# Weights of a tap product side by side in SBUF: a new layout for the tap factors of an S4 convolution kernel

## The chip, the cores and the metric

The kernel runs on one core of a Trainium2 chip. The metric is the device time of one execution in microseconds (us), as the median of several runs. A second number: the mean granted clock of the matmul engine (TensorE, "PE" in the profile). It is read from a record in the trace, as a share of full speed. In the records it takes only two values, 1.0 and 0.5. It begins late, 27.1 us after the first instruction in the kernel before, and the profile counts the time before that as full clock. So all mean clocks and half-clock times below say nothing about the first 30 us or so.

Some terms: SBUF is the on-chip memory that holds the operands, and PSUM the one to which matmuls write their sums. In the profile DVE is the vector engine, ACT the scalar engine, PE a matmul (of a moving operand, whose columns are counted below, with weights loaded before) and PEld the loading of its weights.

Runs of one kernel differ by up to 3%. A run is called slow when it is more than 1.5% above the fastest run of the same kernel. Ratios here use fast runs only.

## The reference, cut to what matters

The reference normalises the input, and runs a diagonal state-space model (S4) as a long convolution. It adds an expert's output for one routed token, applies a gate and adds the residual. The part that this change touches is the generation of the convolution kernel `K`:

```python
logdA = dt * A                              # A complex, (512, 128)
P = jnp.exp(logdA[:, :, None] * l)          # l = 0 .. 2047
K = jnp.einsum("dn,dnl,dn->dl", Cc, P, dB).real
# ... y = irfft(rfft(xn) * rfft(K)) + xn * Dskip
```

The kernel writes the exponential as a product of a factor for a small step (32 steps) and a factor for a large one (20 of them). The factors for the small steps are a table `QQ`, and those for the large steps, together with `C` and `dB`, a table `GG`. Both have the 128 states on the partitions. A matrix product of the two, summed over the states, gives taps of `K`: one such tap product has as its 128 weights the 32 small steps of 4 channels (one channel `jj` of each of the four groups `gp`), and as its 80 moving columns the 20 large steps of the same 4 channels. The exponents of the small steps are themselves made on PE, as outer products of the rows of `dt * A` (a row is a channel) with the numbers 0.5 to 15.5.

## The kernel before

All matmuls are issued through one helper, so the profile gives them all the line L187; its groups are told apart by the names of the operands. A matmul is written `(output in PSUM, weights, moving operand, start, stop)`. `sap(tensor, first partition, partitions, offset, [[step, count], ...])` is an access pattern along the free dimension, in elements. `PB` is the PSUM (float32, 4 bytes an element). The other operands are bfloat16, 2 bytes an element.

The outer products, in 16 calls of `args` (8 from `exps`, 8 from `qgen`):

```python
IDIJ[pp, :, pp % 32] = np.arange(16) + 0.5      # table [128, 16, 32]: 16 numbers, each 32 times to pick a row (channel)

def args(pi, c, pair):
    q, js = c // 2, c % 2
    rs = slice(32 * q, 32 * q + 32)             # 32 rows of the array
    for gp in range(4):
        o = PB[:, 2 * pair + gp // 2, 256 * (gp % 2):256 * (gp % 2) + 256]
        for hl in range(2):                     # high and low half of dt*A
            mms.append((o, AD[rs, pi, hl, gp, :], IDIJ[rs, :, 16 * js:16 * js + 16], hl == 0, hl == 1))
```

One call is 8 matmuls of 256 columns. The moving operand runs over 16 neighbouring elements (32 bytes) at a time, and the PSUM write is contiguous. In the result the channel is the innermost index, so `QQ` has the shape `[128, 2, 2, 4, 32, 16]`, which ends in group, step and channel `jj`.

The tap products, in 8 calls of `kgen` with 32 matmuls each:

```python
mms.append((PB[:, bank, 80 * k:80 * k + 80],
            sap(QQ, 0, 128, 4096 * qb + 2048 * ci + jj, [[16, 128]]),          # weights: step 16 elements, 32 bytes
            sap(GG, 0, 128, 2560 * ci + 16 * js + jj, [[32, 4], [128, 20]]), ci == 0, ci == 1))   # moving: step 256 bytes
```

The weights of one tap product lie 32 bytes apart. That is what the change is about. Two more groups: `PB<-KT,W` (640 matmuls of the spectrum of `K`) and `PB<-PAB,FA` (512 matmuls of the inverse transform). Both have contiguous weights and a contiguous moving operand.

The kernel issues a few matmuls on constants (`PB<-CA`, from L280) for the sole purpose of keeping PE busy. They are called fillers below.

## Time and profile before

| | before |
|---|---|
| median of 3 runs | 224.8 us (224.78 to 227.97) |
| span and granted clock of the profiled run | 222.4 us, 0.899 |
| PE busy | 188.2 us, 85% of the span |

The page of the kernel before has the busy time of each engine, the granted clock in 40 equal slices (tenths, 9 is 90% or more), and the shares of the engines in the chain of work that ended last:

```profile
PE 188.2 (85%) x2399; PEld 142.4 (64%) x2407; DVE 143.9 (65%) x339; ACT 143.9 (65%) x186; POOL 14.0 (6%) x24
...
PEclk9999999999696769766999999855599999999969
...
PE 54%; DVE 20%; ACT 12%; DMA 7%; issue 2%; SPq 2%; POOL 0%; DVEq 0%; ACTq 0%
```

PE is the busiest engine and leads the chain. A slice is 5.56 us. The clock drops in two places, between about 55 and 105 us (several slices of 6 and 7) and between about 140 and 161 us (8, 5, 5, 5), and once more for 3.4 us near the end. As the clock is either 1.0 or 0.5, a mean of 0.899 means that the record holds (1 - 0.899) / 0.5 * 222.4 = 45 us at half clock. The 9s of the first slices are not measured. The first outer products tell that the clock was low there:

```profile
6.79 3.59 PE L187 MATMUL PB<-CA,AD 32*128 32x256 bf16 x16 [6.79 <-DVE AD L738]
```

They start every 213 ns, as the same matmuls do at half clock later; at full clock it is 109 ns.

The groups view of the kernel before gives, after the bar, busy time in us and the mean ns of one instruction, then the idle time before the group:

```profile
L187 PE MATMUL PB<-KT,W 128*128 128x128 bf16 x640 | 41.3, 222 | 0.8 <-ACT K2T L754 0.3 <-issue 0.2
L187 PE MATMUL PB<-GG,QQ 128*128 128x80 bf16 x256 | 40.3, 326 | 0.7 <-ACT KT L754 0.7
...
L187 PEld LDWEIGHTS PB<-GG,QQ 128*128 128x128 bf16 x256 | 35.7, 147 | 3.1 <-ACT KT L754 1.4 <-issue 0.8
L187 PE MATMUL PB<-CA,AD 32*128 32x256 bf16 x128 | 21.5, 323 | 7.5 <-DVE AD L738 6.8 <-ACT EE L754 0.7
...
L725 DVE TENSOR_TENSOR QQ<-QQ,EE 128x2048 bf16<-128x2048 bf16 x16 | 19.5, 1219 | 0.1
L187 PE MATMUL PB<-PAB,FA 64*128 64x128 bf16 x512 | 17.2, 217 | 2.9 <-DVE PAB L725 2.4 <-ACT ZT L754 0.5
...
L725 DVE TENSOR_TENSOR KP<-GG,QQ 128x128 bf16<-128x128 bf16 x8 | 1.8, 221 | 18.4 <-PE PB L187 18.4
```

A busy time of 41.3 us for 640 matmuls is 65 ns apiece; 222 ns is the time from start to end of one. They overlap in time: at full clock one starts every 56 ns. Dividing the busy time by the number is therefore the way to read the rate: 157 ns for each tap product of 80 columns, 65 ns for each spectrum matmul of 128 columns.

The timeline of PE in the kernel before (start, length, group) shows the rate within one burst:

```profile
97.46 1.97 PE L187 MATMUL PB<-GG,QQ 128*128 128x80 bf16 x12
99.25 0.74 PE L187 MATMUL PB<-KT,W 128*128 128x128 bf16 x10
```

Twelve tap products take 99.25 - 97.46 = 1.79 us, 149 ns each, where spectrum matmuls with more columns start every 56 ns at full clock. The tap products also start every 147 to 150 ns in a stretch (150 to 157 us) where the granted clock is 0.5. So what limits them didn't slow down with the PE clock here.

The timeline of the same kernel, later, shows one call of outer products between two groups:

```profile
111.68 1.04 PE L187 MATMUL PB<-CA,AD 32*128 32x256 bf16 x8
112.65 2.41 PE L187 MATMUL PB<-KT,W 128*128 128x128 bf16 x40
```

The call takes 112.65 - 111.68 = 0.97 us.

The windows view of the kernel before gives the busy time and number of instructions of each engine in a stretch, then the granted clock, the share of DMA and GB/s. These are two of the five stretches that the trace was cut into:

```profile
62.00:107.00 45.00, 44.44 (x457) 35.76 (x459) 22.80 (x45) 24.29 (x38) 0.05 (x1) 0.77 0.41 155
107.00:140.00 33.00, 30.33 (x545) 24.06 (x544) 31.16 (x65) 31.71 (x36) 1.18 (x1) 1.00 0.52 144
```

From 107 to 140 us PE, DVE and ACT are all busy for 30 to 32 of 33 us, at full clock. PE time that is added there can hardly be hidden.

### The profile page before, as it was taken

How to read it: one execution, taken by the hardware profiler on the slowest of the kernel's cores; microseconds unless marked ns; L12 is line 12 of the kernel's file. 1: busy time of each engine (PE TensorE's matmuls, PEld its weight loads, DVE VectorE, ACT ScalarE, POOL GpSimd, SP SyncE). 2: the span in 40 equal slices, each digit the busy share in tenths (PEclk: the TensorE clock that was granted, in tenths of full speed). 3: DMA queues.
4: the chain of work that ended last, by engine and by line, in shares of the span. 5: the costliest groups of instructions: out<-in, count | busy, mean ns of one | idle time of the engine just before them, and what ended most of it. 6: DMA issues, size and time to landing. Idle time of an engine off the chain costs nothing.

```text
span 222.4 us, 5535 instructions
## 1 busy us (share of the span) xinstructions
PE 188.2 (85%) x2399; PEld 142.4 (64%) x2407; DVE 143.9 (65%) x339; ACT 143.9 (65%) x186; POOL 14.0 (6%) x24
## 2 busy tenths in 40 slices
PE   0683987975899999999999978899999999997290
PEld 0453575753277768878877755777676989986030
DVE  3899923799960399640599999823889821434273
ACT  2597798557634679342997999643778535566821
POOL 0090000020110000000000002002000300000000
PEclk9999999999696769766999999855599999999969
DMA  6899920289799733000026576748200091377875
GB/s 178 300 367 388 425 120 3 76 239 328 196 411 425 286 89 103 1 3 0 3 62 176 168 184 213 210 135 199 82 3 1 12 216 31 80 165 233 197 170 138
DMA packets 40666, 36.79 MB, mean 165 GB/s; under 512 B 26593, under 2 KB 35938, under 8 KB 39746
## 3 DMA queue, kind: packets, MB, share of 16 engines
q1 hardware_dynamic: 38178, 22.25, 35.4%
q0 software_dynamic: 2464, 14.19, 17.9%
q8 instruction: 19, 0.31, 0.6%
q14 instruction: 5, 0.04, 0.1%
HBM read 25.95 MB, written 10.49 MB: 164 GB/s over the span
## 4 chain that ended last, share of the span: by engine, by line
PE 54%; DVE 20%; ACT 12%; DMA 7%; issue 2%; SPq 2%; POOL 0%; DVEq 0%; ACTq 0%
PE PB L187 51%; DMA WD<-in_B_w_down_dram 4%; DVE PAB L725 4%; DMA X<-in_A_u_dram 3%; ACT K2T L754 3%; DVE TT L725 3%; ACT XT L957 3%; PE PB L280 2%; DVE T L725 2%; DVE ST L802 2%; ACT AT L754 2%; DVE TF L725 2%; SPq L210 2%; ACT QQ L754 1%; DVE GG L725 1%
## 5 line engine op out<-in xcount | busy, mean ns | idle before, releaser
L187 PE MATMUL PB<-KT,W 128*128 128x128 bf16 x640 | 41.3, 222 | 0.8 <-ACT K2T L754 0.3
L187 PE MATMUL PB<-GG,QQ 128*128 128x80 bf16 x256 | 40.3, 326 | 0.7 <-ACT KT L754 0.7
L187 PEld LDWEIGHTS PB<-KT,W 128*128 128x128 bf16 x640 | 37.2, 99 | 4.7 <-ACT K2T L754 2.1
L187 PEld LDWEIGHTS PB<-GG,QQ 128*128 128x128 bf16 x256 | 35.7, 147 | 3.1 <-ACT KT L754 1.4
L754 ACT ACTIVATE KT<-PB 128x400 bf16<-128x400 f32 (+2 forms) x32 | 15.7, 500 | 26.4 <-PE PB L187 26.4
L187 PE MATMUL PB<-CA,AD 32*128 32x256 bf16 (+1 forms) x192 | 24.4, 309 | 8.2 <-DVE AD L738 7.4
L725 DVE TENSOR_TENSOR PAB<-U,K2T 128x1024 bf16<-128x1024 bf16 x32 | 21.0, 686 | 14.6 <-ACT K2T L754 14.6
L725 DVE TENSOR_TENSOR TT<-GG,ZB 128x512 bf16<-128x512 bf16 (+2 forms) x64 | 27.7, 470 | 0.7
L187 PEld LDWEIGHTS PB<-CA,AD 32*128 32x128 bf16 x192 | 15.5, 114 | 15.4 <-DVE AD L738 7.6
L754 ACT ACTIVATE K2T<-PB 128x1024 bf16<-128x1024 f32 x16 | 16.4, 1024 | 8.0 <-PE PB L187 8.0
L754 ACT ACTIVATE AT<-PB 128x1024 bf16<-128x1024 f32 x16 | 15.8, 1021 | 8.3 <-PE PB L187 6.6
L754 ACT ACTIVATE U<-PB 128x1024 bf16<-128x1024 f32 x16 | 16.4, 1022 | 7.0 <-PE PB L187 6.9
L187 PE MATMUL PB<-PAB,FA 64*128 64x128 bf16 x512 | 17.2, 217 | 2.9 <-DVE PAB L725 2.4
L725 DVE TENSOR_TENSOR QQ<-QQ,EE 128x2048 bf16<-128x2048 bf16 x16 | 19.5, 1219 | 0.1
L187 PEld LDWEIGHTS PB<-PAB,FA 64*128 64x128 bf16 x512 | 14.4, 94 | 5.3 <-DVE PAB L725 2.7
L754 ACT ACTIVATE ZT<-PB 128x1024 bf16<-128x1024 f32 x16 | 16.4, 1027 | 1.5 <-PE PB L187 1.5
L725 DVE TENSOR_TENSOR GG<-TT 128x512 bf16<-128x512 bf16 (+2 forms) x32 | 15.1, 473 | 0.8
L754 ACT ACTIVATE EE<-PB 128x1024 bf16<-128x1024 f32 x16 | 15.4, 1023 | 0.2
L187 PE MATMUL PB<-XN,CB 128*128 128x256 bf16 (+1 forms) x80 | 11.9, 280 | 4.2 <-ACT AT L754 2.8
L187 PE MATMUL PB<-BT,F2T 128*64 128x256 bf16 x128 | 13.7, 354 | 0.5 <-ACT K2T L754 0.5
L725 DVE TENSOR_TENSOR KP<-GG,QQ 128x128 bf16<-128x128 bf16 x8 | 1.8, 221 | 18.4 <-PE PB L187 18.4
L187 PE MATMUL PB<-DD,CB 128*128 128x512 bf16 x32 | 10.3, 416 | 3.4 <-DVE KV L725 2.9
(130 smaller groups left out, 235.3 us busy)
## 6 DMA issues: line engine op xcount, KB each, us to landing
W<-c_w POOLq DMA_DIRECT2D x4, 1280.0 KB, 12.5
scr_a<-AT SPq DMA_DIRECT2D x8, 512.0 KB, 6.2
BT<-scr_a SPq DMA_DIRECT2D x8, 512.0 KB, 5.7
scr_z<-ZT SPq DMA_DIRECT2D x16, 256.0 KB, 2.9
DD<-scr_z SPq DMA_DIRECT2D x6, 512.0 KB, 5.2
XR<-in_A_u_dram POOLq DMA_DIRECT2D x4, 512.0 KB, 6.1
out_dram<-XR SPq DMA_DIRECT2D x8, 256.0 KB, 2.6
X<-in_A_u_dram SPq DMA_DIRECT2D x3, 512.0 KB, 6.8
```

The costliest lines, as they stand in the source:

```text
L187: fns.append(lambda e, o=o, l=l, r=r, st=st, sp=sp, tp=tp: e.matmul(o, lhsT=l, rhs=r, start=st, stop=sp, tile_position=tp, skip_group_chec ...
L210: fns.append(lambda e, dst=dst, src=src: e.dma_start(dst, src))
L280: n.fns = [lambda e, o=o: e.matmul(o, lhsT=lhs, rhs=rhs, start=True, stop=True, tile_position=(0, 0), skip_group_check=True)] * k
L725: g.V(lambda e: e.tensor_tensor(out=o, in0=a, in1=b, op=op), [o], [a, b], n, mode)
L754: nd = g.A(lambda e: e.activation(out=o, in_=i, func=func, **kw), [o], ins, n + (110 if "bias" in kw else 0), after=[ph["pre"]] if tab els ...
L802: g.V(lambda e, b=b: e.bn_stats(ST[:, b, :], X0[:, b, :]), [ST[:, b, :]], [X0[:, b, :]], 512)
L957: g.A(lambda e, pv=pv, xt=xt: e.activation(out=xt, in_=pv, func=ACT.Copy), [XT[:, bq % 2]], [PB[:, bank, :]], 1024)
```

## The change

The intent is to have the 128 weights of one tap product side by side, so that they load without a step. `QQ` becomes `[128, 2, 2, 64, 32]`, where 64 is channel `jj` by group and 32 is the step; the 4 * 32 weights of one `jj` are now neighbours. To write `QQ` in that order without a transposition, the outer products must deliver their results channel by channel, with the steps innermost. Hence 16 matmuls of 128 columns in place of 8 of 256, and a moving operand whose neighbouring elements are 64 bytes apart in the unchanged table `IDIJ`.

```diff
--- before.py
+++ after.py
@@ -668,7 +668,7 @@
         EE = place("EE", [128, 9, 1024], BF16)
         AD = place("AD", [128, 2, 2, 4, 128], BF16)
         o_q = cur[0]
-        QQ = place("QQ", [128, 2, 2, 4, 32, 16], BF16)
+        QQ = place("QQ", [128, 2, 2, 64, 32], BF16)
         WW0 = place("WW0", [128, 2, 256], F32, o_q + 8192)
         ZB0 = place("ZB0", [128, 256], F32, o_q + 8192 + 2048)
         o_g = cur[0]
@@ -850,16 +850,17 @@
             rs = slice(32 * q, 32 * q + 32)
             mms = []
             for gp in range(4):
-                o = PB[:, 2 * pair + gp // 2, 256 * (gp % 2):256 * (gp % 2) + 256]
-                for hl in range(2):
-                    mms.append((o, AD[rs, pi, hl, gp, :], IDIJ[rs, :, 16 * js:16 * js + 16], hl == 0, hl == 1))
+                for h in range(2):
+                    o = sap(PB, 0, 128, 512 * (2 * pair + h) + 16 * gp, [[64, 8], [1, 16]])
+                    for hl in range(2):
+                        mms.append((o, AD[rs, pi, hl, gp, :], IDIJ[rs, :, 16 * js + 8 * h:16 * js + 8 * h + 8].rearrange("p k j -> p j k"), hl == 0, hl == 1))
             g.M(mms)
-            return PAIR4[pair]
+            return PAIR[pair].rearrange("p a b -> p (a b)")
 
         def exps(c, pair=0):
             src = args(0, c, pair)
             for s in range(2):
-                act(EE[:, 2 * (c % 4) + s, :].rearrange("p (a b) -> p a b", a=4), src, ACT.Exp, 1024, scale=(-8.0 if s == 0 else 8.0))
+                act(EE[:, 2 * (c % 4) + s, :], src, ACT.Exp, 1024, scale=(-8.0 if s == 0 else 8.0))
 
         g.sec = "pow"
         for jb in range(2):
@@ -1027,14 +1028,15 @@
             bf = c % 2
 
             def qv(s):
-                return QQ[:, bf, :, :, 16 * s:16 * s + 16, :].rearrange("p x a b c -> p x a (b c)")
-
+                return QQ[:, bf, :, :, 16 * s:16 * s + 16]
+
+            src = src.rearrange("p (a b) -> p a b", b=16)
             e0 = 2 * (c % 4)
             act(qv(1)[:, 0], src, ACT.Sin, 1024, scale=-8.0, bias=HPI)
             act(qv(1)[:, 1], src, ACT.Sin, 1024, scale=8.0)
             ts(EE[:, 8, :], EE[:, e0 + 1, :], -1.0, MUL, 1024, 4)
-            tt(qv(0), qv(1), EE[:, e0, :].rearrange("p (a b) -> p a b", a=4)[:, None].to_broadcast([128, 2, 4, 256]), MUL, 2048, 2)
-            ep = EE[:, e0 + 1:9:7 - e0, :].rearrange("p x (a b) -> p x a b", a=4)
+            tt(qv(0), qv(1), EE[:, e0, :].rearrange("p (a b) -> p a b", b=16)[:, None].to_broadcast([128, 2, 64, 16]), MUL, 2048, 2)
+            ep = EE[:, e0 + 1:9:7 - e0, :].rearrange("p x (a b) -> p x a b", b=16)
             tt(qv(1), qv(1), ep, MUL, 2048, 2)
 
         def gchain(q):
@@ -1064,14 +1066,14 @@
                 for k in range(nj):
                     jj = j0 + k
                     for ci in range(2):
-                        mms.append((PB[:, bank, 80 * k:80 * k + 80], sap(QQ, 0, 128, 4096 * qb + 2048 * ci + jj, [[16, 128]]),
+                        mms.append((PB[:, bank, 80 * k:80 * k + 80], sap(QQ, 0, 128, 4096 * qb + 2048 * ci + 128 * jj, [[1, 128]]),
                                     sap(GG, 0, 128, 2560 * ci + 16 * js + jj, [[32, 4], [128, 20]]), ci == 0, ci == 1))
                 g.M(mms)
                 act(KT[:, j0:j0 + nj].rearrange("p a b c -> p (a b c)"), PB[:, bank, 0:80 * nj], ACT.Copy, 80 * nj)
                 j0 += nj
             kp = KP[:]
             gl = GG[:, 0, :, 19, :].rearrange("p x (g s j) -> p x g s j", g=4, s=2)[:, :, :, js, :]
-            tt(kp, gl, QQ[:, qb, :, :, 31, :], MUL, 128, 1)
+            tt(kp, gl, sap(QQ, 0, 128, 4096 * qb + 31, [[2048, 2], [32, 4], [128, 16]]), MUL, 128, 1)
             mms = []
             for gp in range(4):
                 for m in range(4):
```

## The prediction

> **What bounds the kernel now.** The chain of waits puts 51% of the span on the matmul helper line; PE is busy 85% (page, part 1). The change touches three streams.
>
> 1. Tap products (PB<-GG,QQ, 256 pairs). In the timeline they start every 147 to 150 ns; the 640 pairs PB<-KT,W, whose weights and moving operand are both contiguous, start every 56 ns. The group view shows the weight load at 147 ns against 99. That suggests the strided weights, but neighbouring instructions say otherwise: the last GG matmul before a KT,W matmul (contiguous weights) still holds it back 137 to 138 ns, and a strided QQ load behind a KT,W matmul delays nothing (56 ns). At a burst's start the next load begins 44 ns after a strided one, 15 ns after a contiguous one. So the moving operand GG, 80 columns 256 B apart, sets about 1.7 ns per column, and the strided weights add only about 11 ns. The 149 ns also holds where the granted clock is 0.50 (150 to 157 us), so the limit is in time, not in PE clocks.
> 2. The KT matmuls, moving stride 160 B, agree: a 64-column one holds its successor 101 to 108 ns. The KP matmuls, contiguous moving and a PSUM step of 16 B, follow in 28 ns for 64 columns.
> 3. Step outer products (PB<-CA,AD, 128 matmuls of 256 columns): moving runs of 16 elements, 110 ns at full clock, 213 at half.
>
> **What the change does.** It makes the tap weights contiguous: I expect 137 ns instead of 148, 256 x 11 ns = 2.8 us less PE, nearly all critical. But the outer products become 256 matmuls of 128 columns whose moving operand steps 64 B every column. [...] The 160 B and 256 B streams agree, at 1.6 to 1.7 ns per column; no stream of this trace moves at 64 B, but the weight load at 32 B is slowed too. My estimate is 215 ns per new matmul at either clock: a call of outer products takes 3.44 us instead of 0.88 (1.7 at low clock). DVE and ACT write 16-element runs instead of 256: KP reads such runs in 221 ns today, so I expect no change; KP itself loses some 60 ns.
>
> **Critical path, by calls.** First four calls: PE becomes the limit, 4 x 3.44 us from 6.8 us; ACT reaches the layernorm's logarithm at about 24.5 instead of 19.9: +4.6. Call at 38 us, inside the router's chain: +2.4. Call at 51.7: hidden before the WD load. Calls at 77 and 85: +1.8, +2.4. Stretch 107 to 140 us: PE 30.3, DVE 31.2, ACT 31.7 of 33 us busy; six calls add 15.4 to PE, gaps absorb about 2.6: +12.8. Calls at 154 and 165: +1.8, +2.6. Sum +28.4, less 2.8: about +25.6. I add a little for lower granted clock.
>
> **Prediction: 251 us, range 242 to 262; faster 0.04, same 0.04, slower 0.92.**
>
> **What would show it.** PB<-CA,AD matmuls starting 215 ns apart; their busy time near 55 us instead of 21.5; GG matmuls 135 to 140 ns apart, their weight loads near 100 ns; QQ TENSOR_TENSOR still about 1.22 us; PE, not DVE, leading the chain between 110 and 140 us.
>
> **What would make it wrong.** If a 64 B step runs at full rate, the outer products stay near 56 ns per 128 columns and the result is about 222 us. If GG pairs fall toward 60 ns, the weight load was the limit after all, worth up to 20 us. [...]

The 215 ns stand as an estimate from the streams of the trace: at the 1.58 to 1.71 ns a column of the 160- and 256-byte steps, 128 columns take 202 to 219 ns.

## The result and the profile after

| | before, same rounds | after |
|---|---|---|
| median | 224.79 us (4 runs, 222.51 to 227.97) | 266.92 us (4 runs, 263.08 to 267.96) |
| ratio of fast runs | | 1.18, 95% interval 1.158 to 1.205 |
| span and clock of the profiled run | 222.4 us, 0.899 | 266.0 us, 0.775 |

A ratio is the mean time of one kernel's fast runs over that of the other's fast runs of the same rounds, so it isn't quite the ratio of the medians quoted. The output was correct, here and in every experiment below.

The kernel is slower, as predicted, but by 42 us (by the medians; 41 us by the fast runs) instead of 26. The result is outside the predicted range. The profiled run of the kernel after (267.52 us) counts as slow; its two fast runs took 263.08 and 266.32 us at a clock of 0.821 and 0.793. Every run of the kernel after, fast or slow, had a lower clock than 0.83, so the low clock isn't a trait of the profiled run alone. As that run is 2.8 us above the mean of the two fast ones, the times of its trace below are a little too high.

The page of the kernel after, same lines:

```profile
PE 240.1 (90%) x2527; PEld 164.6 (62%) x2535; DVE 145.6 (55%) x339; ACT 145.4 (55%) x186; POOL 14.0 (5%) x24
...
PEclk9999998557965589779795559556558799799957
...
PE 81%; ACT 11%; DVE 3%; DMA 2%; issue 1%; SPq 0%; DVEq 0%; ACTq 0%
```

PE gained 52 us of busy time and leads 81% of the chain. The row of the clock has changed more than anything else: half clock is now spread over the whole run from the seventh slice on. It adds up to (1 - 0.775) / 0.5 * 266.0 = 120 us. The mean clocks of the two fast runs give 94 and 110 us in the same way.

The groups of the kernel after:

```profile
L187 PE MATMUL PB<-CA,AD 32*128 32x128 bf16 x320 | 59.6, 367 | 7.1 <-DMA CA<-c_ca 7.1
L187 PE MATMUL PB<-KT,W 128*128 128x128 bf16 x640 | 49.8, 246 | 1.0 <-issue 0.3 <-ACT K2T L754 0.3
...
L187 PE MATMUL PB<-GG,QQ 128*128 128x80 bf16 x256 | 37.6, 314 | 0.7 <-ACT KT L754 0.7
...
L187 PEld LDWEIGHTS PB<-GG,QQ 128*128 128x128 bf16 x256 | 28.9, 117 | 7.1 <-ACT KT L754 1.4 <-issue 1.1
...
L187 PE MATMUL PB<-PAB,FA 64*128 64x128 bf16 x512 | 20.8, 242 | 1.4 <-DVE PAB L725 1.4
L725 DVE TENSOR_TENSOR QQ<-QQ,EE 128x2048 bf16<-128x2048 bf16 x16 | 19.5, 1220 | 0.6 <-ACT QQ L754 0.4
...
L725 DVE TENSOR_TENSOR KP<-GG,QQ 128x128 bf16<-128x128 bf16 x8 | 3.0, 369 | 17.1 <-PE PB L187 17.1
```

The group `PB<-CA,AD 32x128` now holds 64 matmuls of another step (the powers, 3.9 us before) as well as the 256 new outer products. The outer products grew from 21.5 to about 59.6 - 3.9 = 55.7 us. Tap products fell from 40.3 to 37.6 us. The surprise is in the second and the fifth line: `PB<-KT,W` grew from 41.3 to 49.8 us and `PB<-PAB,FA` from 17.2 to 20.8 us, though the change doesn't touch them.

The timeline of the kernel after, at the place that was shown of before:

```profile
111.70 1.81 PE L187 MATMUL PB<-GG,QQ 128*128 128x80 bf16 x12
113.33 0.74 PE L187 MATMUL PB<-KT,W 128*128 128x128 bf16 x10
```

Twelve tap products now take 1.63 us, 136 ns each. And the calls of outer products, with the group behind them:

```profile
125.49 3.62 PE L187 MATMUL PB<-CA,AD 32*128 32x128 bf16 x16
129.05 4.03 PE L187 MATMUL PB<-KT,W 128*128 128x128 bf16 x40
...
134.20 2.41 PE L187 MATMUL PB<-KT,W 128*128 128x128 bf16 x40
```

A call takes 129.05 - 125.49 = 3.56 us, or 223 ns a matmul with the handover; inside the burst they start every 216 ns. The 40 spectrum matmuls that follow took 2.41 us before and take 4.03 us here. The next 40, at 134.20, take 2.41 us again: the same instructions, at another clock (0.5 in the record from 129.25 to 132.66 us, 1.0 from there to 139.49 us).

Windows of the kernel after, for the corresponding stretches:

```profile
71.40:121.00 49.60, 48.95 (x480) 35.08 (x481) 23.47 (x45) 24.95 (x39) 0.41 (x1) 0.72 0.36 134
121.00:176.20 55.20, 55.08 (x587) 37.88 (x582) 31.89 (x66) 32.73 (x35) 1.18 (x1) 0.70 0.37 101
```

The busy stretch of 33.0 us has become 55.2 us, in which PE is busy all but 0.1 us and the granted clock is 0.70. With the five stretches of both traces, cut at the same events, the gain and loss by stretch is as follows:

| stretch in before, us | before | after | change | predicted |
|---|---|---|---|---|
| 0 to 21 | 21.0 | 24.8 | +3.8 | +4.6 |
| 21 to 62 | 41.0 | 46.6 | +5.6 | +2.4 |
| 62 to 107 | 45.0 | 49.6 | +4.6 | +2.8 |
| 107 to 140 | 33.0 | 55.2 | +22.2 | +12.8 |
| 140 to 222.4 | 82.4 | 89.8 | +7.4 | +3.0 |

(The predicted column puts half of the 2.8 us gained by the tap products into each stretch that has them.) The early stretch, which the record of the clock doesn't reach, came out slightly better than predicted. Each of the others came out worse; their recorded clock is 0.78, 0.72, 0.70 and 0.79 after, against 0.96, 0.77, 1.00 and 0.87 before.

The groups with contiguous operands that the change left alone explain where PE time appeared from: `KT,W` +8.5, `PAB,FA` +3.6, `XN,CB` +3.0, `DD,CB` +2.2, `BT,F2T` +0.8 and the fillers +1.5 us of busy time. That is 19.6 us. The tap products, which start every 136 to 139 ns in the kernel after at full and at half clock alike, show no such growth.

### The profile page after: what moved, and what is told of

The parts are those of the page before. It is cut to its first block, busy times and chain, and to the rows that moved or that the text cites. A ratio compares the mean times of both kernels' runs of the same rounds, so it can differ in the third digit from the quotient of the medians.

```text
span 266.0 us, 5791 instructions
## 1 busy us (share of the span) xinstructions
PE 240.1 (90%) x2527; PEld 164.6 (62%) x2535; DVE 145.6 (55%) x339; ACT 145.4 (55%) x186; POOL 14.0 (5%) x24
## 4 chain that ended last, share of the span: by engine, by line
PE 81%; ACT 11%; DVE 3%; DMA 2%; issue 1%; SPq 0%; DVEq 0%; ACTq 0%
PE PB L187 78%; ACT K2T L754 2%; PE PB L280 2%; ACT AT L754 2%; ACT XT L958 2%; DMA CA<-c_ca 2%; DVE TF L725 1%; ACT QQ L754 1%; ACT EE L754 1%; ACT XN L754 1%; PE PB L955 1%; ACT EP L754 1%; DVE XR L725 1%; DVE PAB L725 0%; SPq L210 0%
## 5 line engine op out<-in xcount | busy, mean ns | idle before, releaser
L187 PE MATMUL PB<-CA,AD 32*128 32x128 bf16 x320 | 59.6, 367 | 7.1 <-DMA CA<-c_ca 7.1
L187 PEld LDWEIGHTS PB<-CA,AD 32*128 32x128 bf16 x320 | 30.1, 115 | 33.3 <-DVE AD L738 7.1
L187 PE MATMUL PB<-KT,W 128*128 128x128 bf16 x640 | 49.8, 246 | 1.0 <-issue 0.3
L187 PEld LDWEIGHTS PB<-KT,W 128*128 128x128 bf16 x640 | 45.1, 112 | 6.0 <-issue 3.0
L187 PE MATMUL PB<-GG,QQ 128*128 128x80 bf16 x256 | 37.6, 314 | 0.7 <-ACT KT L754 0.7
L187 PEld LDWEIGHTS PB<-GG,QQ 128*128 128x128 bf16 x256 | 28.9, 117 | 7.1 <-ACT KT L754 1.4
L754 ACT ACTIVATE KT<-PB 128x400 bf16<-128x400 f32 (+2 forms) x32 | 15.7, 499 | 25.6 <-PE PB L187 25.6
L754 ACT ACTIVATE K2T<-PB 128x1024 bf16<-128x1024 f32 x16 | 16.4, 1026 | 17.5 <-PE PB L187 17.4
L187 PE MATMUL PB<-PAB,FA 64*128 64x128 bf16 x512 | 20.8, 242 | 1.4 <-DVE PAB L725 1.4
L187 PEld LDWEIGHTS PB<-PAB,FA 64*128 64x128 bf16 x512 | 17.7, 107 | 4.5 <-issue 1.7
L725 DVE TENSOR_TENSOR QQ<-QQ,EE 128x2048 bf16<-128x2048 bf16 x16 | 19.5, 1220 | 0.6 <-ACT QQ L754 0.4
L725 DVE TENSOR_TENSOR TF<-PB,XN 128x512 bf16<-128x512 f32 x12 | 8.3, 690 | 17.6 <-PE PB L187 12.2
L187 PE MATMUL PB<-XN,CB 128*128 128x256 bf16 (+1 forms) x80 | 15.0, 330 | 2.8 <-ACT KV L754 1.2
```

What stands on the lines that cost most here:

```text
L187: fns.append(lambda e, o=o, l=l, r=r, st=st, sp=sp, tp=tp: e.matmul(o, lhsT=l, rhs=r, start=st, stop=sp, tile_position=tp, skip_group_chec ...
L725: g.V(lambda e: e.tensor_tensor(out=o, in0=a, in1=b, op=op), [o], [a, b], n, mode)
L754: nd = g.A(lambda e: e.activation(out=o, in_=i, func=func, **kw), [o], ins, n + (110 if "bias" in kw else 0), after=[ph["pre"]] if tab els ...
```

## The experiments

Three questions were open.

1. Is it the 64-byte step of the moving operand that makes the outer products slow (my theory), or the shorter matmuls, the tap layout and what follows from it (rivals)?
2. What are the limits of the rate: the moving operand's step, the weights' step, the PSUM step?
3. Where do the further 16 us come from: from the lower clock (theory), or from waits and engine order that follow from longer calls whatever the clock (rival)? And what lowers the clock: the slow steps, or the long use of only 32 of the 128 rows?

Some of the texts speak of stalls. They mean the extra time of a stepped matmul (216 ns instead of 56); no trace shows what PE does in it.

All times are given beside runs of the kernel before on the same chip. That kernel's own fast runs range from 222 to 225 us.

### e1_table: the same layout, with a table that makes the moving operand contiguous

From the kernel after; the table is stored the other way round, nothing else is changed.

```diff
-    IDIJ = np.zeros((128, 16, 32))
+    IDIJ = np.zeros((128, 32, 16))
-        IDIJ[pp, :, pp % 32] = np.arange(16) + 0.5
+        IDIJ[pp, pp % 32, :] = np.arange(16) + 0.5
-        IDIJ = cbv("IDIJ").rearrange("p (b c) -> p b c", b=16)
+        IDIJ = cbv("IDIJ").rearrange("p (b c) -> p b c", b=32)
-   ... IDIJ[rs, :, 16 * js + 8 * h:16 * js + 8 * h + 8].rearrange("p k j -> p j k") ...
+   ... IDIJ[rs, 16 * js + 8 * h:16 * js + 8 * h + 8, :] ...
```

> The change with one thing undone: the constant table of step midpoints is stored tap by tap (32 taps x 16 steps), so the moving operand of the outer products is 128 neighbouring elements; order of results, layout of the tap factors and all other engines stay as in the change. If the 64 B step of the moving operand is the whole cost: outer products 54 to 56 ns apart per 128 columns at full clock (107 at half), tap products 138 ns as in the change, mean clock near 0.90, time 220 to 223 us, some 1 to 2 per cent under the kernel before. If the order of results (runs of 16 columns in PSUM, 16-element runs on VectorE and ScalarE, twice as many matmuls) costs by itself: 230 us or more.

Measured: 220.69 us (6 runs, 218.92 to 221.35), ratio 0.990 (0.984 to 0.996), clock 0.919. Two groups of its profile:

```profile
L187 PE MATMUL PB<-GG,QQ 128*128 128x80 bf16 x256 | 37.6, 314 | 0.9 <-ACT KT L754 0.7 <-DVE GG L725 0.3
...
L187 PE MATMUL PB<-CA,AD 32*128 32x128 bf16 x320 | 24.6, 256 | 9.1 <-DVE AD L738 7.5 <-ACT EE L754 1.6
```

The outer products need 24.6 - 3.9 = 20.7 us and start every 57 ns at full clock. The tap products keep their gain. So all of the loss hangs on the step of the moving operand, and none on the shorter matmuls, on the tap layout or on the runs of 16 elements that DVE and ACT now write. This version is faster than both kernels, by about 1% over before. That is a small gain: the interval excludes equality, but it doesn't reach the 2% at which a verdict would be "faster". It agrees with the 2.7 us that the tap products gained.

### e2_psumstep: the step moved from the moving operand to the PSUM write

From the kernel after; the moving operand runs over 8 neighbouring elements (16 bytes), and the output is written with a step of 64 floats instead.

```diff
-   o = sap(PB, 0, 128, 512 * (2 * pair + h) + 16 * gp, [[64, 8], [1, 16]])
+   o = sap(PB, 0, 128, 512 * (2 * pair + h) + 16 * gp, [[1, 16], [64, 8]])
-   ... IDIJ[rs, :, 16 * js + 8 * h:16 * js + 8 * h + 8].rearrange("p k j -> p j k") ...
+   ... IDIJ[rs, :, 16 * js + 8 * h:16 * js + 8 * h + 8] ...
```

> The change with the table as it was, but the moving operand read in the table's own order (runs of 8 neighbouring elements) and the reordering done on the write: the results go to PSUM with a step of 256 B. If a PSUM step costs nothing (the KP matmuls of before suggest it): 54 to 58 ns per matmul, time equal to the run with the reordered table, 220 to 224 us. If a PSUM step slows matmuls[...]: about 215 ns per matmul and a time like the changed kernel's, 260 us or more.

Measured: 235.38 us (232.96 to 236.24), ratio 1.057 (1.047 to 1.066), clock 0.901. Its outer products and powers:

```profile
L187 PE MATMUL PB<-CA,AD 32*128 32x128 bf16 x320 | 42.1, 358 | 7.3 <-DVE AD L738 7.0 <-ACT EE L754 0.2
```

The matmuls start every 107 to 109 ns at full clock and every 206 to 213 ns at half clock. A PSUM write with this step takes twice the time of a contiguous one here (56 ns at full clock, 107 at half), and unlike the moving operand's step (216 ns at either clock) it does slow down with the clock. Neither of the two expectations came true. This refutes the reading in my prediction that a PSUM step is free. That reading came from the `KP` matmuls, which write only four partitions; why they follow in 28 ns isn't settled here.

### e4_stepsonly: the slow outer products alone, in the kernel before

From the kernel before, with its tap layout, its 256 columns and its strided weights; only the order of the outer products is turned, with the output put where the kernel before expects it.

```diff
-                o = PB[:, 2 * pair + gp // 2, 256 * (gp % 2):256 * (gp % 2) + 256]
+                o = sap(PB, 0, 128, 512 * (2 * pair + gp // 2) + 256 * (gp % 2), [[1, 16], [16, 16]])
-   ... IDIJ[rs, :, 16 * js:16 * js + 16] ...
+   ... IDIJ[rs, :, 16 * js:16 * js + 16].rearrange("p k j -> p j k") ...
```

> The kernel before (tap factors in their old layout) with one thing from the change: the 256-column outer products read their constant with a 64 B step. It also writes PSUM with a 64 B step, to keep the old order of results. If the stepped read is the whole loss of the change: about 430 ns per 256 columns, time 265 to 272 us, a little above the changed kernel because the tap products keep 148 ns. If the change's other parts (16-element runs, twice as many matmuls) carry some of the loss: below 258 us.

Measured: 264.95 us (4 runs, 262.89 to 268.29), ratio 1.184 (1.174 to 1.193). The profiled run is a slow one, at a clock of 0.800. Two of its groups:

```profile
L187 PE MATMUL PB<-CA,AD 32*128 32x256 bf16 x128 | 55.9, 604 | 6.9 <-DVE AD L738 6.9
...
L187 PE MATMUL PB<-GG,QQ 128*128 128x80 bf16 x256 | 40.3, 327 | 0.7 <-ACT KT L754 0.7
```

The outer products need 55.9 us, as after the change, and the tap products 40.3 us, as before it. The loss is the same as that of the whole change (1.18). (e4 writes PSUM with a step as well, but the probe below shows that this adds nothing to so slow a read: 232 ns with and without.) With e1 this answers the first question from both sides: without the step the loss is gone, and with the step alone it is whole.

### e6_probe: the rates by themselves

The kernel before, with 27 bursts of 24 identical matmuls added behind its last PE work. They read data at hand and their results are read by nobody.

```diff
+        def probe():
+            X = lambda free, p=128: sap(XN0, 0, p, 0, free)
+            cases = [(o, IDENT, X([[s, 128]])) for s in (1, 2, 4, 8, 16, 32, 64)]   # moving step
+            ...                                     # runs, PSUM steps, weight steps, 32 rows
+            for c in cases:
+                g.M([(c[0], c[1], c[2], True, True)] * 24)
```

> The kernel before, with 27 bursts of 24 identical matmuls added after its last one (results not used), to measure each stream by itself: moving operand with a step of 1, 2, 4, 8, 16, 32, 64 elements of 2 bytes; runs of 2, 4, 8, 16 elements with gaps; 32 rows instead of 128; PSUM steps of 8, 16 and 256 B; weights with a step of 1 to 32 elements under a short moving operand. [...]steps of 1, 2, 4 elements near 56 ns at full clock, 8 and more near 215 ns, alike for 32 and 128 rows[...]. If the cost grows with the step instead: 16 below 32 below 64. Weights with a step of 16 elements: 44 to 60 ns per pair, contiguous 25 to 30 ns. PSUM step of 256 B: 107 ns at full clock, as the run with stepped PSUM writes showed; a step of 16 B should show the same if any step does.

One run, 301.48 us, which means nothing here. What counts is the median distance between the starts of neighbouring matmuls, read from the trace. The moving operand has 128 columns of 2 bytes, if nothing else is said.

| varied | distance, ns |
|---|---|
| contiguous | 56 at full clock, 107 at half |
| moving step 4 / 8 / 16 / 32 / 64 / 128 bytes | 58 / 116 / 227 / 232 / 217 / 218 (the first two at full clock, the third at full and then half clock, the others at half) |
| moving step 64 bytes, 32 rows instead of 128 | 217 at either clock |
| moving: 2 neighbours, then to the next 16 bytes | 116 (at half clock) |
| moving: 4 neighbours in every 32 bytes | 107 (at half clock) |
| moving: runs of 8 or 16 neighbours | 56 (at full clock) |
| PSUM step 8 / 16 / 256 bytes | 213 at half clock / 109 at full, 214 at half / 213 at half |
| moving step 32 bytes and PSUM step 256 bytes | 232 |
| weights' step 2 / 4 / 8 / 16 / 32 / 64 bytes, 16 columns moving | 25 / 25 / 33 / 60 / 62 / 57 (the first four at full clock, the last at half) |
| 80 columns at 64 bytes, weights contiguous / step 32 bytes | 137 / 145 |

At full clock a moving step of 4, 8 and 16 bytes took 58, 116 and 227 ns, against 56 for a contiguous operand. From 16 bytes on it makes little difference whether the step is 16 or 128 bytes (217 to 232 ns), and at 64 bytes none how many rows are used or what the clock is (217 ns with 32 and with 128 rows; the kernel after has 216 ns at both clocks). Pairs of neighbours with a gap took 116 ns at half clock, where a contiguous operand takes 107 ns, so there they cost little. For a step of 8 bytes I had expected the full rate of 56 ns, and was wrong about that, too.

Each PSUM step of the table (8, 16 and 256 bytes) took twice the time of a contiguous write: 109 ns at full clock (16 bytes) and 213 to 214 at half. But not every write that isn't contiguous costs: in e1 runs of 16 neighbours (64 bytes), 256 bytes apart, ran at 57 ns.

The last row explains the tap products: with weights at 32 bytes they took 149 ns in the kernel before and 136 to 138 ns after, against 145 and 137 ns here. The moving operand `GG`, with its step of 256 bytes, sets the rate, and the weights' step adds about 10 ns.

### e7_six and e8_sixfill: the same PE time, slow or full of fillers

These two answer whether the further loss is the clock. Both start from e1. In e7 the six calls between 107 and 140 us are slow again (moving step of 32 bytes, PSUM step of 256 bytes, 231 ns a matmul). In e8 the same six calls run at full rate, behind 13 fillers of 512 columns, so that they take about as long.

```diff
 e7_six
+            slow = c >= 4 and (pi == 0 or c < 6)
+                    if slow:
+                        mv = mv.rearrange("p j k -> p k j")
+                        o = sap(PB, 0, 128, 512 * (2 * pair + h) + 16 * gp, [[1, 16], [64, 8]])
 e8_sixfill
+            if c >= 4 and (pi == 0 or c < 6):
+                mms = [(PB[:, 2 * pair + k % 2, :], IDENT, CA[:, 0:512], True, True) for k in range(13)]
```

> The corrected kernel (table stored tap by tap, 220.7 us) with the slow read put back in six calls only: the four step outer products for the second set of exponentials and the first two behind it, all in the stretch that lay at 107 to 140 us in the kernel before. They read with a 32 B step, which the probe measured at 232 ns per 128 columns (64 B: 217), so a call takes 3.71 us instead of 0.89: 6 x 2.82 = 16.9 us more PE time. With my slack of 2.6 us and an unchanged clock: about 235 us. Theory (the clock falls because of the stalls and the neighbours run at half rate): 240 to 247 us, clock under 0.86. Rival (my slack is wrong, the clock has no part): about the same time as the twin run with fillers.

> Twin of the run with six slow calls: in the same six calls the read is fast and 13 filler matmuls of 128x128 by 512 columns (216 ns each, 2.81 us) stand in front of it, so PE is held as long but streams all the time. Theory: 233 to 237 us, clock 0.90 or more. Rival (only the length of a call counts): the same time as the twin, whatever that is.

Measured: e7 247.83 us (247.14 to 247.92), ratio 1.106 (1.092 to 1.120), clock 0.818. e8 237.02 us (236.79 to 238.03), ratio 1.060 (1.045 to 1.074), clock 0.890. The granted clock and part of the timeline of e7:

```profile
PEclk9999999995975895598875569775557999999869
```

```profile
111.34 3.87 PE L187 MATMUL PB<-CA,AD 32*128 32x128 bf16 x16
115.14 4.00 PE L187 MATMUL PB<-KT,W 128*128 128x128 bf16 x40
```

And of e8:

```profile
PEclk9999999995877597559999999976679999999769
```

```profile
111.19 2.98 PE L187 MATMUL PB<-CA 128*128 128x512 bf16 x13
114.10 1.06 PE L187 MATMUL PB<-CA,AD 32*128 32x128 bf16 x16
115.09 2.41 PE L187 MATMUL PB<-KT,W 128*128 128x128 bf16 x40
```

The call takes 115.14 - 111.34 = 3.80 us in e7 and 115.09 - 111.19 = 3.90 us in e8, and the same 40 spectrum matmuls follow. They take 4.00 us behind the slow call and 2.41 us behind the fillers. In e7 the clock is down for most of the stretch that follows (8, 8, 7, 5, 5 and 6 tenths in the row above, from 111 to 148 us); in e8 it is full (nines from 106 to 153 us). Over the whole run `KT,W` needs 48.4 us in e7 and 41.8 us in e8:

```profile
L187 PE MATMUL PB<-KT,W 128*128 128x128 bf16 x640 | 48.4, 242 | 0.8 <-ACT K2T L754 0.3
L187 PE MATMUL PB<-KT,W 128*128 128x128 bf16 x640 | 41.8, 224 | 0.7 <-ACT K2T L754 0.3
```

The difference in time, 247.83 - 237.02 = 10.8 us, is what the lost clock costs, as the calls are equally long within about 0.1 us. The rival (waits and order, whatever the clock) would have made e8 as slow as e7, and falls.

Both runs came out just above the times that I expected (240 to 247 and 233 to 237 us), and e8 just below the clock (0.890 instead of 0.90 or more). Against e1, e8 is about 16 us longer by the ratios, for 6 * 2.91 = 17.5 us of fillers. Less the 2.6 us of gaps in the prediction that would be 14.9 us, which the noise of the ratios (some 3.5 us) doesn't tell apart.

### e5_early: the first four calls alone

From e1 with `slow = pi == 0 and c < 4`; the rest is as in e7, against which the line is shown.

```diff
-            slow = c >= 4 and (pi == 0 or c < 6)
+            slow = pi == 0 and c < 4
```

> The corrected kernel with the slow read (232 ns) in the first four calls only, where the granted clock is at half anyway. By my sum of the prediction 220.7 + 4.6 + about 1 for the 32 B step = 226 us; if these calls lie behind the load of X and cost nothing: 221 us. No change of the clock expected from 30 us on.

Measured: 226.0 us (224.72 to 229.71, the highest a slow run), ratio 1.006 (0.982 to 1.030), clock 0.907. Over e1 that is 5.3 us for the four calls whose cost I predicted as 4.6 us. (The calls of e5 are at 232 ns a matmul, a bit slower than those of the change. That the clock is at half there isn't in the record; it was read from the 213 ns of the first outer products in the kernel before.) But e1 ran on another chip, and by the ratios of the two runs to the kernel before it is 3.5 us. The interval is wide; the early term is right in size, no more can be said.

### e3_dense and e3b_rows32: two failed attempts

Both were to give the later twelve calls the PE time of the kernel after at full array use (e3, fillers) or in 32 rows without a slow step (e3b, four times as many matmuls). Both were made from the kernel after, with the output step of e2 to get a contiguous moving operand.

```diff
+                    mv = IDIJ[rs, :, 16 * js + 8 * h:16 * js + 8 * h + 8]
+                    if pi == 0 and c < 4:
+                        mv = mv.rearrange("p k j -> p j k")
+                    else:
+                        o = sap(PB, 0, 128, 512 * (2 * pair + h) + 16 * gp, [[1, 16], [64, 8]])
 e3_dense: 12 fillers ahead of each such call;  e3b_rows32: for hl in (0, 1) * 4
```

> The PE time of the change without its stalls: the first four calls as in the change, the other twelve use contiguous reads, each behind 12 filler matmuls of 128x128 by 512 columns, so that a call still takes about 3.5 us at full clock but streams all the time. Theory (the missing 16 us come from the lower granted clock that stalled streaming brings): mean clock 0.88 or more, KT,W busy near 41 us as before, time 246 to 254 us. Rival (the added PE time costs more on the critical path than my sum by calls, whatever the clock): 262 to 268 us with a clock of 0.88 or more.

> As the run with fillers, but a call is stretched by repeating its own contiguous matmuls four times (64 matmuls of 32 rows by 128 columns, about 3.5 us at full clock). If the clock follows how steadily columns stream, it stays near 0.88 and the time near 246 to 254 us. If it follows how much of the array works (32 of 128 rows), the clock falls to 0.80 or less although nothing stalls, calls take up to 7 us in the low state, and the time is 265 us or more.

Measured: e3 261.56 us, ratio 1.172 (1.161 to 1.183), clock 0.908. e3b 356.16 us, ratio 1.584 (1.563 to 1.606), clock 0.727. Neither tells anything about the question. I had taken the PSUM step for free, and e2, which ran beside them, showed that it isn't. The calls of e3 took 12 fillers (2.6 us) and 16 * 107 ns, 4.3 us in all and not 3.5; those of e3b took 9 to 14 us. They were made again on e1, where the output lies in runs of 16 neighbours.

### e3c_dense: the PE time of the change with the clock kept

From e1: the first four calls slow, the other twelve at full rate behind 12 fillers. They were meant to take 3.5 us a call; in the trace it is 3.7 us at full clock.

```diff
+            slow = pi == 0 and c < 4
+            if not slow:
+                mms = [(PB[:, 2 * pair + k % 2, :], IDENT, CA[:, 0:512], True, True) for k in range(12)]
```

> The run with fillers once more, without the stepped PSUM write that made its calls 0.8 us too long: first four calls slow (232 ns per matmul), the other twelve read contiguously behind 12 fillers of 216 ns, 3.5 us per call at full clock, as long as a call of the change. The run with only the four early slow calls took 226.0 us; my prediction's terms for the other twelve sum to 23.8 us. If the sum by calls was right and only the clock was missing from it: 247 to 253 us with a clock of 0.88 or more, against 267 us for the change. If the sum was too low by itself: 262 us or more.

Measured: 251.96 us (251.5 to 254.23), ratio 1.128 (1.118 to 1.139), clock 0.917. Clock and groups of its profile:

```profile
PEclk9999999999977699756999999997599999999859
```

```profile
L187 PE MATMUL PB<-KT,W 128*128 128x128 bf16 x640 | 41.3, 222 | 0.9 <-ACT K2T L754 0.3
...
L187 PE MATMUL PB<-CA 128*128 128x512 bf16 x144 | 37.6, 416 | 0.2 <-ACT EE L754 0.2
...
L187 PE MATMUL PB<-CA,AD 32*128 32x128 bf16 x320 | 29.7, 267 | 6.8 <-DVE AD L738 6.8
```

`KT,W` needs 41.3 us, exactly as before the change. With the clock kept, the loss is 12.8%, or 0.128 * 224.8 = 29 us, where the prediction had 26 us. The whole change loses 18.15%, or 41 us. The missing 12 us are the clock; the 95% intervals of the two ratios leave some 6 us of doubt either way. The 10.8 us of e7 and e8 are of the same order, but not the same quantity, as only six calls differ there.

### e3d_rows32: 32 rows at full rate

From e1: in the later twelve calls each matmul is issued four times (64 contiguous matmuls of 32 rows instead of 16). The last pair of each sum still starts anew, so the result is right.

```diff
+            slow = pi == 0 and c < 4
-                    for hl in range(2):
+                    for hl in (0, 1) * (1 if slow else 4):
```

> First four calls slow (232 ns), the other twelve contiguous and repeated four times: 64 matmuls of 32 rows by 128 columns, 56 ns each at full clock, 3.6 us per call, without any stalls. If stalls are what lowers the clock: clock near 0.9, time 246 to 254 us. If a long stretch that uses 32 of 128 rows lowers it as well: clock 0.8 or less, calls up to 6.8 us, time 262 us or more; then the slow read is not the only way to lose the clock.

Measured: 276.51 us (272.84 to 279.41, the highest a slow run), ratio 1.239 (1.216 to 1.262), clock 0.817. Two calls in its timeline:

```profile
164.86 3.74 PE L187 MATMUL PB<-CA,AD 32*128 32x128 bf16 x64
...
193.16 7.00 PE L187 MATMUL PB<-CA,AD 32*128 32x128 bf16 x64
```

The first has 64 matmuls in 3.74 us, 58 ns each as at full clock, and is as long as a slow call. The second, the same work at 109 ns each as at half clock, takes 7.00 us. A call that is caught at half clock nearly doubles and keeps PE in the same low use for longer. So slow outer products aren't needed for losing the clock (0.817 over the run; only the first four calls of e3d are slow, all before 22 us). Perhaps 32 rows aren't either: the tap products of the kernel before use 128 rows at a slow step, and sit in one of its half-clock stretches (143 to 160 us), though a call of outer products lies there too. Both fit a reading of mine, that the clock follows how much of the array works rather than how long PE has an instruction in flight; these runs don't decide it.

A count over the traces of before and after goes with it. For each whole period of 3.41 us in the two records (the step in which the clock changes), add up the columns of the matmuls that started in it, each weighted with its share of the 128 rows. A cut at 3060 such columns tells in 111 of 124 periods (90%) whether the next period was at full or at half clock. Columns without the weight, cut at 3580, tell it in 103 (83%), and "as in this period" in 85 (69%). The cuts were set on these same traces. This describes them and is no experiment, and it fails in one period of ten; what the clock follows isn't shown.

## Why the prediction was right or wrong

Point by point, with the prediction's words first.

- "So the moving operand GG ... sets about 1.7 ns per column, and the strided weights add only about 11 ns": right. Expected 137 ns, measured 136 to 138 ns in the burst; 40.3 to 37.6 us of busy time, against 2.8 us predicted. The probe shows the same with other data. The weight loads came out at 117 ns, not "near 100 ns".
- "My estimate is 215 ns per new matmul at either clock": right. 216 ns in the burst, 217 ns in the probe at both clocks. The busy time of the outer products is 55.7 us against "near 55 us". What carried it were the trace's own streams at 160 and 256 bytes, at 1.6 to 1.7 ns a column.
- "KP matmuls ... PSUM step of 16 B, follow in 28 ns", which I took to say that a PSUM step is free: wrong as a general statement (e2, e6). It wasn't in the sum, but it cost two experiments.
- "I expect no change" of DVE and ACT writing runs of 16 elements: right, QQ on DVE went from 1219 to 1220 ns. "KP itself loses some 60 ns": it lost 148 ns (221 to 369), eight times in a run, 1.2 us on DVE in all.
- The critical path by calls: its sum is right within a few us when the clock is kept; the terms weren't tested one by one. e3c, which adds this PE time at full array use, lost 29 us against the predicted 26. The first term, "+4.6", measured +3.8 in the kernel after. "Call at 51.7: hidden" is doubtful: the stretch from 21 to 62 us lost 5.6 us, not 2.4, at a clock that fell from 0.96 to 0.78 there; what share of it was that call isn't settled.
- "I add a little for lower granted clock": this is the step that failed. It stood for 251 - (224.8 + 25.6) = 0.6 us. It was worth about 12 us: 40.8 us of loss in the kernel after against 28.8 us in e3c; the pair e7 and e8 lost 10.8 us to it in six calls. Half-clock time in the record went from 45 to 120 us (94 to 110 us in the fast runs), and 19.6 us of PE busy time was added to contiguous matmuls that the change didn't touch. Part of that fell into time in which PE had been idle, so less shows in the span.

The prediction knew that the new matmuls run at 215 ns at either clock, and expected PE to lead the chain in the busiest stretch. It gave no reason for the "little", and in effect took the clock of the matmuls that were not changed as given. In the worst stretch PE was busy for 55.08 of 55.2 us and had a mean clock of 0.70. The clock in the two records takes only two values, full and half, and changes only at multiples of 3.41 us from the record's start. But a busy share near one didn't go with full clock. The kernel before already had a hint: in its half-clock stretch from 143 to 160 us, which holds tap products, PE was busy all the time (17.06 of 17.06 us).

## What to carry to other kernels

Before a layout is turned for the benefit of one operand, find out who pays with a step: a moving operand with a step of 16 to 128 bytes ran at a quarter of the full-clock rate here (217 to 232 ns instead of 56), and strided weights of a matmul that is limited elsewhere cost about 10 ns of 149; here a constant table could be stored the other way round, and nobody paid. Cost a slow PE stream twice, once for its own time and once for the clock of what runs behind it (10.8 us between e7 and e8 here), and to separate the two, replace it by the same time of full-rate matmuls on all rows. When matmuls that a change didn't touch have become slower, look at the granted clock first (here `KT,W` went from 41.3 to 49.8 us as the mean clock fell from 0.899 to 0.775).
